# One whole matmul for two half-wide ones in the last Fourier stage of the first batch, with its pieces placed later

## The chip, the cores and the metric

The kernel runs on one core of a Trainium2 chip, as one launch. The metric is the device time of that core in microseconds, median of three runs. A core has five engines with queues of their own: TensorE (PE in the profile; its weight loads are PEld), VectorE (DVE), ScalarE (ACT), GpSimd (POOL) and SyncE (SP, which here only starts DMA transfers). Each works through its queue in order, and they wait for one another through semaphores. Operands lie in SBUF, which has 128 partitions; TensorE writes to PSUM, and DVE and ACT empty PSUM ("evacuate" it).

## The reference

Eight batches of 3008 tokens with 256 channels pass through a global filter (a real Fourier transform along the tokens, a product with a complex filter, the inverse transform) and then through a two-layer network whose activation is h + sin²(αh)/α:

```python
def _attn_ref(x, filt_r, filt_i):                 # x: (8, 3008, 256)
    X = np.fft.rfft(x, axis=1)
    F = (filt_r + 1j * filt_i)[None, :, :]
    return np.fft.irfft(X * F, n=x.shape[1], axis=1).astype(np.float32)

def _moe_ref(x, w_in, w_out, alpha):              # x: (24064, 256), w_in: (256, 2048)
    h = x @ w_in
    s = np.sin(alpha * h)
    g = h + s * s / (alpha + 1e-09)
    return (g @ w_out).astype(np.float32)
```

## The kernel before

**The transform.** 3008 = 94 x 32, and the transform is done in steps of matrix products with tables: a first stage over 94 rows, a forward stage over the other index, the product with the filter, an inverse stage, and a last stage that gives back rows of 94 tokens. Results are fp16 in SBUF.

**Batches 1 to 7** (class `Spectral`) go through DRAM between the stages to turn the data: `first` (L180 matmul, L161/L159 evacuation, store to `d1` on SP), `load_t2` (POOL), `forward` (L200), `product` and `cross` (DVE; the copies `xs` between them are started by SP), `inverse` (L231), `load_t4`, and `last`. Their last stage is L258: four matmuls a piece, each with 128 adjacent columns of `t4_h` as weights and 94 columns of a table as the moving operand.

**Batch 0** is done first, by code of its own, without DRAM in between. Its data stand as pairs of channels, two fp16 values in four bytes, so that DVE's 32x32 transpose (`turn`, L385) can turn pairs as 32-bit words. `pairs(t)` is the view of a tile as partition, s (32), channel pair, k (2): neighbouring channel pairs of one s lie 64 elements (128 bytes) apart, and the two members of a pair lie side by side. The stages:

- 16 matmuls `pa_0` (L371), evacuated by DVE and ACT in turn into `t1_0` as pairs of the channels 2c and 2c+1
- four transposes into `t2_0`, one half of the channels (`hc`) after the other
- twelve blocks of `forward_0` (L403, four matmuls a block over 64 pairs of one half, evacuated by ACT at L407), `product_0` (L412, DVE) and `inverse_0` (L422, eight matmuls a block, evacuated by ACT at L159 into `g_0` as pairs of c and c+64 within the half). Six forward blocks run ahead of the inverse ones; from then on each round has one inverse and one forward block
- `turn_back` (L385, two transposes of 2048 words) into `t4_0`, one half each. These tiles are `t4_h`, which earlier hold half of the turned data (`t2_0[0]`) and the second inverse table (`e1_0`)
- the last stage, 16 pieces `s0.last(u)` of 4 x 94 columns of `y` for 128 channels (L255). A piece takes eight matmuls: for each of four s, the member k of 64 pairs gives the weights, 64 columns wide, and the result goes to PSUM partitions 64k to 64k+63. A piece with `cb` = 0 needs the first `turn_back` alone, one with `cb` = 1 the second. PSUM buffers come from the pool `fps`, which has two. The evacuation goes to ACT or DVE (`on_act`)

`warm_pe(n)` puts n matmuls without use into the queue. `weights_in` (POOL) multiplies the first weights by alpha; `weights_out` (POOL, and ACT for the last four) the second weights by -1/(2 alpha), which `reciprocals` makes from `rec` with a TensorE transpose and a DVE operation.

**The MLP** walks over 48 chunks of up to 512 tokens, 8 steps a chunk. A step issues two hidden blocks (`hidden`: two matmuls at L507, the cosine on ACT at L510, the combination on DVE at L511) and, for the chunk before, projections (`project`, L523; in the first chunk there are none). Hidden blocks have four PSUM buffers (`hps`).

**The order around the change** is written out by hand. `put(at, function)` files a piece of Fourier work under a step number; after the hidden blocks of a step and again after its projections, `slot(step)` and `slot(step + 0.5)` issue what is due, as a rule one piece with matmuls at a time, a second one only when it is a whole step late. Four pieces of batch 0's last stage are issued before the MLP begins; the others are filed in pairs (`last_two`, one piece evacuated by ACT and one by DVE). Chunk 2 (steps 16 to 23) is the first to read pieces 6 to 9.

Of the kernel before, what the change touches and what calls it, by code (L numbers as in the profile page):

```python
# [9 lines left out]
FP16 = mybir.dt.float16  # L10
# [4 lines left out]
ALU = mybir.AluOpType  # L15
# [3 lines left out]
B, S, C = 8, 3008, 256  # L19
# [43 lines left out]
def kernel(  # L63
# [10 lines left out]
    nc = tc.nc  # L74
# [17 lines left out]
    def pool(name, bufs, space=None):  # L92
        kw = {} if space is None else {"space": space}
        return ctx.enter_context(tc.tile_pool(name=name, bufs=bufs, **kw))

    cpool = pool("consts", 1)
# [12 lines left out]

    wf_t = cpool.tile([NR, NK], FP16)  # L110
    t1_h = [cpool.tile([128, 16, C], FP16, name=f"t1_h{i}") for i in range(2)]
    t4_h = [cpool.tile([128, 16, C], FP16, name=f"t4_h{i}") for i in range(2)]

    def by_half(t):

# [8 lines left out]
    for h in range(2):  # L124
        nc.sync.dma_start(out=x32[:, 4 * C * h:4 * C * h + 4 * C],
                          in_=bass.AP(tensor=x.tensor, offset=x.offset + 4 * h * C, ap=[[32 * C, 96], [1, 4 * C]]))
# [4 lines left out]
    wi0_t = cpool.tile([128, NR], FP16)  # L131
    filt_t = cpool.tile([128, 2, NS, C], FP16)
# [23 lines left out]
    def evac(dst, src, on_act=None):  # L156
        flip[0] = (flip[0] + 1) % 3
        if flip[0] if on_act is None else on_act:
            marks["act"] = nc.scalar.copy(out=dst, in_=src)  # L159
        else:  # L160
            marks["dve"] = nc.vector.tensor_copy(out=dst, in_=src)  # L161

    class Spectral:
# [82 lines left out]
        def last(self, u, on_act=None):  # L246
            ch, rest = divmod(u, 4)
            half, cb = divmod(rest, 2)
            n0 = 8 * ch + 4 * half
            ps = fps.tile([128, 4, 128], FP32, name=f"pd_{self.b}_{u}", tag="f")  # L250
            psv = ps.rearrange("p a b -> p (a b)")[:, 0:4 * NR].rearrange("p (a r) -> p a r", r=NR)
            for i in range(4):
                if self.b == 0:
                    for k in range(2):
                        nc.tensor.matmul(out=psv[64 * k:64 * k + 64, i, :], lhsT=t4_0[cb][:, n0 + i, :, k],  # L255
                                         rhs=wi0_t, start=True, stop=True)
                else:
                    nc.tensor.matmul(out=psv[:, i, :], rhs=wi_t, start=True, stop=True,  # L258
                                     lhsT=t4_h[ch // 2][0:NK, n0 % 16 + i, cb * 128:cb * 128 + 128])
            evac(y[:, cb, self.b % 2, n0:n0 + 4, :], psv, on_act)  # L260
# [9 lines left out]
    al = cpool.tile([16, 128], FP32)  # L270
# [33 lines left out]
    for g in range(2):  # L304
        gs = slice(12 * g, 12 * g + 12)
        for k, filt in enumerate((filt_r, filt_i)):
            for q in range(2):
                if (g, k, q) == (0, 1, 1):
# [3 lines left out]
                    out=f_t[k][64 * k + 32 * q:64 * k + 32 * q + 32, gs, :],  # L312
                    in_=bass.AP(tensor=filt.tensor, offset=filt.offset + off,
                                ap=[[N1 * C, 32], [step, 12], [1, C]]))
# [6 lines left out]
    def pairs(t):  # L321

        return t.rearrange("p a (b s k) -> p s (a b) k", s=32, k=2)

    t1_0 = vpool.tile([128, 32, C], FP16, name="t1_0", tag="v")
    t2_0 = [t4_h[0], vpool.tile([128, 16, C], FP16, name="t2_0", tag="v")]
    for hc in range(2):
        nc.vector.memset(pairs(t1_h[hc])[:, NS:32], 0.0)
    t1_0, t2_0, g_0, t4_0 = pairs(t1_0), [pairs(t) for t in t2_0], [pairs(t) for t in t1_h], [pairs(t) for t in t4_h]
    rec = cpool.tile([16, 128], FP32)  # L330
    rec_t = cpool.tile([128, 16], FP32)
# [17 lines left out]
    def warm_pe(n):  # L349

        warmed.append(n)
        ps = hps.tile([128, 512], FP32, name=f"warm_{len(warmed)}", tag="h")
        for i in range(n):
            nc.tensor.matmul(out=ps, lhsT=idle[:, 0:128], rhs=idle[:, 0:512], start=True, stop=True)
# [7 lines left out]
    def cast_x0(h):  # L362

        cs = slice(4 * C * h, 4 * C * h + 4 * C)
        evac(x0[0].rearrange("p n c -> p (n c)")[:, cs], x32[0:NR, cs], False)

    cast_x0(0)
    for i in range(16):
        own, tag = (fps, "f") if i % 3 == 2 else (hps, "h")
        ps = own.tile([128, 512], FP32, name=f"pa_0_{i}", tag=tag)  # L370
        nc.tensor.matmul(out=ps, lhsT=wf0_t[0:NR], rhs=x0[i // 4][:, 2 * (i % 4):2 * (i % 4) + 2, :],  # L371
                         start=True, stop=True)
        evac(t1_0[:, 2 * i:2 * i + 2], ps.rearrange("p (n c k) -> p n c k", n=2, k=2), i % 2)
        if i == 1:
            warm_pe(3)
            cast_x0(1)
        if i < 15 and i % 4 == 3:
            warm_pe((2, 2, 2, 1)[i // 4])
# [9 lines left out]
    def turn_back(hc):  # L388

        turn(t4_0[hc], g_0[hc])  # L390
# [6 lines left out]
    xf0, p0 = {}, {}  # L397

    def forward_0(i):
        hc, w = blocks[i]  # L400
        ps = hps.tile([128, 4, 128], FP32, name=f"pb_0_{i}", tag="h")
        for j in range(4):
            nc.tensor.matmul(out=ps[:, j, :], lhsT=d_t[:, 4 * w + j, :],  # L403
                             rhs=t2_0[hc][:, 4 * w + j], start=True, stop=True)
        own, tag = (xspool, "xs") if i % 2 else (xfpool, "xf")
        xf0[i] = own.tile([128, 4, 128], FP16, name=f"xf_0_{i}", tag=tag)
        nc.scalar.copy(out=xf0[i], in_=ps)  # L407

    def product_0(i):
        hc, w = blocks[i]  # L410
        p0[i] = xpool.tile([128, 2, 4, 128], FP16, name=f"p_0_{i}", tag="x")
        marks["products"] = nc.vector.tensor_tensor(  # L412
            out=p0[i], in0=xf0[i][:, None].to_broadcast([128, 2, 4, 128]),
            in1=filt_t[:, :, 4 * w:4 * w + 4, 128 * hc:128 * hc + 128], op=ALU.mult)

    def inverse_0(i):
        hc, w = blocks[i]
# [36 lines left out]
    s0 = Spectral(0)  # L454

    [inverse_table(g) for g in range(2)]
    for i in range(6):
        forward_0(i)
        if i % 3 == 2:
            if i == 2: inverse_table(2)  # L460
            warm_pe((4, 0)[i // 3])
    for i in range(13):
        for e in {5: [(1,0,False)],6: [(1,1,False)]}.get(i, ()):
            other_half(*e)
        if i < 12:
            product_0(i)
        if i > 0:
            inverse_0(i - 1)
        if i + 6 < 12:
            forward_0(i + 6)  # L470
        if i == 12:
            turn_back(0)
    turn_back(1)
    nc.vector.reciprocal(out=rec, in_=al)
    def weights_out(jb, n=4):

        if n == 1:
            nc.scalar.mul(w2[:, jb, :], w_out32[:, jb, :], rec_t[:, jb:jb + 1])
        else:
            nc.gpsimd.tensor_tensor(out=w2[:, jb:jb + n, :], in0=w_out32[:, jb:jb + n, :],  # L480
                                    in1=rec_t[:, jb:jb + n, None].to_broadcast([128, n, C]), op=ALU.mult)
# [2 lines left out]
    spread_alpha(3)  # L484
    for step in ([(weights_in, g) for g in range(6)] + [(s1.load_x, 0), (s1.load_x, 1)]):
        step[0](*step[1:])
    warm_pe(2)
    s0.last(0, True)
    s0.last(2, True)
    warm_pe(3)  # L490
    s0.last(1, True)
    s0.last(3, False)

    chunks = [(pb, c0, 384 if c0 == 2560 else 512) for pb in range(B // 2)
              for c0 in [*range(0, 2561, 512), *range(2944, 2 * S, 512)]]
# [61 lines left out]
    def put(at, fn, *args, pe=False):  # L557
        pending.append((at, len(pending), pe, fn, args))
# [10 lines left out]
    for i in range(2):  # L569
        put(13 + i, negate, i)  # L570
    for u in range(4, 16, 2):
        put((1,3,4.5,6,14,16)[u // 2 - 2], s0.last_two, u, pe=True)
    for b in range(1, B):
        s = s1 if b == 1 else Spectral(b)
        z = 48 * b
        if b > 1:
            for ch in range(4):
                put((22,27,32,37)[ch] if b == 2 else z - 92 + 7 * ch, s.load_x, ch)
        for i in range(16):
            put(7.5 + 0.3 * i if b == 1 else 36 + 0.66 * i if b == 2 else z - 67 + 0.66 * i, s.first, i, pe=True)  # L580
        for g in range(4):
            put(12.5 if b == 1 else max(z - 56, 46.5), s.load_t2, g)
        for u in range(12):
            inv = 23.5 + 1.25 * u if b == 1 else 59 + 2.1 * u if b == 2 else z - 40.8 + 2.3 * u
            fwd = inv - (6 if b == 1 else 6)
            put(fwd, s.forward, u, pe=True)
            put(fwd + (0.5 if b == 1 else 1.5), s.product, u)
            if s.fused:
                put(fwd + (4 if b == 1 else 4.5), s.cross, u)
            put(inv, s.inverse, u, pe=True)  # L590
        for ch in range(4):
            put(z - (9.5 if b == 1 and ch < 3 else (10.5, 10.5, 10.5, 3)[ch]), s.load_t4, ch)
        for u in range(16):
            put(z + (u - (5 if b == 1 else 6.5) if u < 4 else 2 * u - 9), s.last, u, pe=True)
# [68 lines left out]
```

## Time and profile before

| | us |
|---|---|
| median of three runs | 790.48 (790.2 to 791.0) |
| span of the profiled execution | 789.0 |
| TensorE busy in the span | 776.2 |
| VectorE busy | 657.4 |
| ScalarE busy | 617.0 |
| GpSimd busy | 79.7 |
| L255, 128 matmuls of 64 wide weights | 9.8 |
| L403, 48 matmuls | 6.6 |

The span runs from the first instruction of the program to the last; the time of a run has some work around it, here 1.48 us between the span and the median. A busy TensorE is an upper bound, because matmuls overlap and their ends are modelled; where the distance between starts is known, it is the better price. "L255" is line 255 of the kernel.

### The profile page before, as it was taken

To read this page: it belongs to the slowest core of one execution; us is meant where nothing else is said; L and a number is where in the kernel's file an instruction comes from. 1 tells how busy PE (TensorE), PEld (TensorE's weight loads), DVE (VectorE), ACT (ScalarE), POOL (GpSimd) and SP (SyncE) were. 2 spreads that over 40 slices of the span, in tenths; PEclk is the share of its full clock that TensorE was granted. 3 is DMA by queue.
4 is the path that set the end of the run, shared out by engine and by line. 5 is a ranking of instruction groups with operands and counts; after the bars stand their busy time and mean duration, and the time that the engine had idled before them with its cause. 6 is when DMAs were issued, how large, how long until landed. Compare 5 with 4: busy or idle time off the path is not lost.

```text
span 789.0 us, 16730 instructions
## 1 busy us (share of the span) xinstructions
PE 776.2 (98%) x5854; PEld 536.3 (68%) x5854; DVE 657.4 (83%) x1171; ACT 617.0 (78%) x1209; POOL 79.7 (10%) x125
## 2 busy tenths in 40 slices
PE   8999989999999999999999999999999999999997
PEld 4756757676667766777666766777666776766666
DVE  7887987899878997799978998799987999777773
ACT  6887868888878887888887888788887887777663
POOL 6442000200020000200020000200002000000000
PEclk9999999999999999999999999999999999999999
DMA  9956568755573646554575455845566233421111
GB/s 217 257 105 173 118 144 206 173 104 134 140 198 82 135 98 191 150 121 102 121 210 124 100 106 137 219 94 113 128 165 171 62 97 82 116 62 29 41 41 54
DMA packets 87677, 101.01 MB, mean 128 GB/s; under 512 B 14472, under 2 KB 75928, under 8 KB 87592
## 3 DMA queue, kind: packets, MB, share of 16 engines
q1 hardware_dynamic: 78016, 73.73, 34.5%
q0 software_dynamic: 9360, 26.15, 17.4%
q8 instruction: 46, 0.75, 0.4%
q14 instruction: 39, 0.32, 0.1%
q10 hardware_dynamic: 216, 0.05, 0.0%
HBM read 55.72 MB, written 46.66 MB: 130 GB/s over the span
## 4 chain that ended last, share of the span: by engine, by line
PE 90%; DVE 2%; DMA 2%; ACT 2%; issue 1%; POOL 1%; SPq 1%; ACTq 0%; POOLq 0%; DVEq 0%
PE po L523 40%; PE ph L507 40%; PE pa L180 3%; PE pd L258 2%; PE pb L200 2%; PE pc L231 2%; DMA e_t<-e_tbl 1%; DVE v L511 1%; PE pd L255 1%; DMA xs<-xf 1%; ACT cos_all L510 1%; DVE t_h L385 1%; SPq L549 1%; ACT t_h L159 1%; DVE t_h L161 0%
## 5 line engine op out<-in xcount | busy, mean ns | idle before, releaser
L511 DVE SCALAR_TENSOR_TENSOR v<-cos_all,ph 128x512 f16<-128x512 f32 (+1 forms) x768 | 482.8, 671 | 107.4 <-ACT cos_all L510 103.9
L510 ACT ACTIVATE cos_all<-ph 128x512 f32<-128x512 f32 (+1 forms) x768 | 410.9, 592 | 99.5 <-PE ph L507 98.3
L523 PE MATMUL po<-w,v 128*128 128x256 f16 x3008 | 388.7, 272 | 0.0
L507 PE MATMUL ph<-y,w 128*128 128x512 f16 (+1 forms) x1536 | 386.4, 374 | 0.5 <-DVE y L161 0.3
L523 PEld LDWEIGHTS <-v 128*128 128x128 f16 x3008 | 289.3, 98 | 78.2 <-issue 1.2
L507 PEld LDWEIGHTS <-w 128*128 128x128 f16 x1536 | 147.5, 98 | 104.5 <-issue 2.5
L529 ACT COPY o<-po 128x512 f32<-128x512 f32 (+1 forms) x97 | 55.6, 573 | 19.6 <-PE po L523 12.6
L203 ACT CAST xf<-pb 128x512 f16<-128x512 f32 x84 | 50.0, 595 | 15.2 <-PE pb L200 13.8
L192 POOL DMA_DIRECT2D t<-d x56 | 36.3, 666 | 202.4 <-DMA out_dram<-o 128.6
L159 ACT CAST t_h<-pa 96x512 f16<-96x512 f32 x74 | 43.3, 586 | 8.5 <-PE pa L180 8.3
L140 POOL DMA_DIRECT2D x<-in_x_dram x32 | 17.1, 535 | 302.1 <-PE pc L231 171.4
L159 ACT CAST y<-pd 128x376 f16<-128x376 f32 x83 | 40.0, 482 | 7.6 <-PE pd L258 5.3
L258 PEld LDWEIGHTS <-t_h 96*128 96x128 f16 x448 | 31.4, 97 | 18.4 <-issue 0.4
L180 PE MATMUL pa<-x,wf_t 94*96 94x512 f16 x112 | 42.2, 381 | 1.0 <-DVE t_h L161 0.6
L159 ACT CAST g<-pc 128x512 f16<-128x512 f32 x58 | 34.4, 593 | 9.4 <-PE pc L231 9.0
L221 DVE TENSOR_TENSOR p<-p,xs 128x512 f16<-128x512 f16 x84 | 35.7, 425 | 2.9
L220 DVE TENSOR_TENSOR xs<-xs,filt_t 128x512 f16<-128x512 f16 x84 | 35.0, 416 | 2.8 <-DMA xs<-xf 2.8
L258 PE MATMUL pd<-wi_t,t_h 96*128 96x94 f16 x448 | 37.1, 204 | 0.0
L214 DVE TENSOR_TENSOR p<-xf,filt_t 128x512 f16<-128x512 f16 x84 | 35.0, 416 | 0.0
L231 PE MATMUL pc<-p,e_t 128*128 128x256 f16 x168 | 32.1, 273 | 1.7 <-DVE p L221 1.7
L200 PE MATMUL pb<-t,d_t 128*128 128x256 f16 x168 | 32.1, 272 | 0.5 <-DVE g L161 0.4
L161 DVE CAST t_h<-pa 96x512 f16<-96x512 f32 x38 | 25.9, 681 | 0.7 <-PE pa L180 0.5
(66 smaller groups left out, 257.5 us busy)
## 6 DMA issues: line engine op xcount, KB each, us to landing
x<-in_x_dram POOLq DMA_DIRECT2D x30, 376.0 KB, 5.0
d<-t_h SPq DMA_DIRECT2D x28, 384.0 KB
t<-d POOLq DMA_DIRECT2D x56, 192.0 KB, 4.6
xs<-xf SPq DMA_DIRECT2D x168, 64.0 KB
d<-g SPq DMA_DIRECT2D x56, 192.0 KB
t_h<-d SPq DMA_DIRECT2D x28, 384.0 KB
out_dram<-o SPq DMA_DIRECT2D x104, 80.0 KB
w_out<-in_moe_w_out_dram SPq DMA_DIRECT2D x1, 2048.0 KB
```

What stands on the lines that cost most here:

```text
L159: marks["act"] = nc.scalar.copy(out=dst, in_=src)
L180: marks["pe"] = nc.tensor.matmul(out=ps[0:NK, :], lhsT=wf_t, rhs=self.x[ch][:, 2 * j:2 * j + 2, :], start=True, stop=True)
L192: nc.gpsimd.dma_start(out=self.t2[g][64 * p:64 * p + 64, :, :], in_=self.d1[a0:a0 + 6, :, :].rearrange("s n c -> n s c"))
L200: nc.tensor.matmul(out=ps[:, i, :], lhsT=d_t[:, s, :], rhs=self.t2[s // 6][:, s % 6, :], start=True, stop=True)
L203: nc.scalar.copy(out=self.xf[u], in_=ps)
L231: nc.tensor.matmul(out=ps[:, i, :], lhsT=e_t[:, 2 * w + i, :], rhs=pt[:, i, :], start=(k == 0), stop=(k == len(pr) - 1))
L258: nc.tensor.matmul(out=psv[:, i, :], rhs=wi_t, start=True, stop=True, lhsT=t4_h[ch // 2][0:NK, n0 % 16 + i, cb * 128:cb * 128 + 128])
L507: nc.tensor.matmul(out=ps[:, 0:n], lhsT=w1[:, cb, jb * 128:jb * 128 + 128], rhs=y_cols[:, cb, c0:c0 + n], start=(cb == 0), stop=(cb == 1))
L510: nc.scalar.activation(out=cs[:, 0:n], in_=ps[:, 0:n], func=AFT.Sin, bias=float(np.pi / 2))
L511: marks["snake"] = nc.vector.scalar_tensor_tensor(out=v[k][:, jb, 0:n], in0=cs[:, 0:n], scalar=-1.0, in1=ps[:, 0:n], op0=ALU.add, op1=ALU. ...
L523: nc.tensor.matmul(out=pso[k][:, t % 2, :], lhsT=v[k][:, jb, 128 * t:128 * t + 128], rhs=w2[:, jb, :], start=(jb == 0), stop=(jb == 15))
L529: nc.scalar.copy(out=o[:, i0:t % 2 + 1, :], in_=pso[k][:, i0:t % 2 + 1, :])
```

## The change

The diff does five things. The pairs of batch 0 become the channels c and c+128 (the evacuation of `pa_0`, the order in which `forward_0` reads, the columns of the filter in `product_0`). Both halves of `t4` become one tile, so that one member k of all 128 pairs can be the weights of one matmul, and a piece takes four matmuls rather than eight. With that every piece needs both `turn_back` transposes; the four early pieces are issued in order, with ACT and DVE in turn, after eight warm matmuls in one group, and the reciprocal is issued after them on DVE. The pairs of pieces from 4 on are filed at 2, 5, 13, 14.5, 16 and 17.5 rather than at 1, 3, 4.5, 6, 14 and 16. Batch 1's first stage is filed from 7.9 rather than from 7.5.

```diff
-    t4_h = [cpool.tile([128, 16, C], FP16, name=f"t4_h{i}") for i in range(2)]
+    t4_a = cpool.tile([128, 2, 16, C], FP16)
+    t4_h = [t4_a[:, i] for i in range(2)]
...
                 if self.b == 0:
-                    for k in range(2):
-                        nc.tensor.matmul(out=psv[64 * k:64 * k + 64, i, :], lhsT=t4_0[cb][:, n0 + i, :, k],
-                                         rhs=wi0_t, start=True, stop=True)
+                    nc.tensor.matmul(out=psv[:, i, :], lhsT=t4_cols[:, n0 + i, :, cb], rhs=wi0_t,
+                                     start=True, stop=True)
...
+    t4_cols = t4_a.rearrange("p h a (b s k) -> p s (h a b) k", s=32, k=2)
...
-        evac(t1_0[:, 2 * i:2 * i + 2], ps.rearrange("p (n c k) -> p n c k", n=2, k=2), i % 2)
+        evac(t1_0[:, 2 * i:2 * i + 2], ps.rearrange("p (n k c) -> p n c k", n=2, k=2), i % 2)
...
-                             rhs=t2_0[hc][:, 4 * w + j], start=True, stop=True)
+                             rhs=t2_0[hc][:, 4 * w + j].rearrange("p c k -> p k c"), start=True, stop=True)
...
-            out=p0[i], in0=xf0[i][:, None].to_broadcast([128, 2, 4, 128]),
-            in1=filt_t[:, :, 4 * w:4 * w + 4, 128 * hc:128 * hc + 128], op=ALU.mult)
+            out=p0[i].rearrange("p f s (k c) -> p f s k c", k=2),
+            in0=xf0[i].rearrange("p s (k c) -> p s k c", k=2)[:, None].to_broadcast([128, 2, 4, 2, 64]),
+            in1=filt_t[:, :, 4 * w:4 * w + 4].rearrange("p f s (k c) -> p f s k c", k=2)[..., 64 * hc:64 * hc + 64],
+            op=ALU.mult)
...
-    nc.vector.reciprocal(out=rec, in_=al)
...
-    warm_pe(2)
-    s0.last(0, True)
-    s0.last(2, True)
-    warm_pe(3)
-    s0.last(1, True)
-    s0.last(3, False)
+    warm_pe(8)
+    for u in range(4):
+        s0.last(u, u % 2 == 0)
+    nc.vector.reciprocal(out=rec, in_=al)
...
-        put((1,3,4.5,6,14,16)[u // 2 - 2], s0.last_two, u, pe=True)
+        put((2,5,13,14.5,16,17.5)[u // 2 - 2], s0.last_two, u, pe=True)
...
-            put(7.5 + 0.3 * i if b == 1 else 36 + 0.66 * i if b == 2 else z - 67 + 0.66 * i, s.first, i, pe=True)
+            put(7.9 + 0.3 * i if b == 1 else 36 + 0.66 * i if b == 2 else z - 67 + 0.66 * i, s.first, i, pe=True)
```

## The prediction

> **What bounds the kernel now.** I read the page first, then the chain of waits in order of time over the first 75 us, then the timeline of the matmuls that the change touches, then the busy times of the first MLP chunk.
>
> The page (busy microseconds, share of the span, number of instructions; then the chain that ended last):
>
> ```profile
> span 789.0 us, 16730 instructions
> PE 776.2 (98%) x5854; PEld 536.3 (68%) x5854; DVE 657.4 (83%) x1171; ACT 617.0 (78%) x1209; POOL 79.7 (10%) x125
> PE 90%; DVE 2%; DMA 2%; ACT 2%; issue 1%; POOL 1%; SPq 1%; ACTq 0%; POOLq 0%; DVEq 0%
> ```
>
> TensorE is busy 98% and is 90% of the chain. What moves the end is therefore either matmul time in the saturated part or delay ahead of it. The chain (start, length, what):
>
> ```profile
> 11.77 9.71 DMA e_t<-e_tbl
> 21.53 0.64 PE pc L422 x8
> ...
> 29.75 0.61 ACT t_h L159
> 30.38 4.51 DVE t_h L385 x2
> 34.94 1.23 PE pd L255 x16
> 36.19 0.56 DVE y L161
> 36.79 0.82 PE ph L507 x3
> ...
> 65.79 1.11 PE pd L255 x15
> 70.48 1.09 PE pd L255 x16
> ```
>
> Until 21.53 us the chain is a DMA (`e_t`). Then come the evacuations of the first batch's inverse stage (L159), the two `turn_back` transposes (L385), the first four pieces of the last stage (L255) and the MLP, which begins to flow at 36.79. Pieces 12 to 15 (at 65.79 and 70.48) lie on the chain by themselves, some 1.1 us a pair of pieces.
>
> The timeline (start, duration, engine, line; "xN" merges N equal instructions, and the duration includes the last one's latency):
>
> ```profile
> 15.70 1.49 PE L403 MATMUL pb<-t_h,d_t 128*128 128x128 f16 x12
> 17.12 0.64 PE L343 MATMUL pse<-id,d_t 128*64 128x128 f16 x16
> 17.69 1.04 PE L354 MATMUL warm<-idle 128*128 128x512 f16 x4
> 21.99 0.60 PE L403 MATMUL pb<-t,d_t 128*128 128x128 f16 x4
> 22.41 0.23 PE L422 MATMUL pc<-p,e_t 128*128 128x128 f16 x1
> 38.68 1.23 PE L255 MATMUL pd<-wi_t,t_h 128*64 128x94 f16 x16
> 137.60 0.33 PE L258 MATMUL pd<-wi_t,t_h 96*128 96x94 f16 x4
> ```
>
> The busy times of the first MLP chunk (stretch, its length; PE, weight loads, DVE, ACT, POOL busy with their instructions; granted clock, DMA share, GB/s):
>
> ```profile
> 36.79:50.13 13.34, 12.52 (x97) 7.40 (x98) 10.55 (x19) 10.48 (x22) 10.60 (x9) 1.00 0.73 152
> ```
>
> Three prices follow. L403 streams 128 columns as 64 adjacent pairs, each pair 128 bytes from the next: (1.49 - 0.29) / 11 = 0.11 us a matmul. L422 streams 128 adjacent columns: the eight of the chain give (0.64 - 0.22) / 7 = 0.06. L255 runs its 64-wide halves two and two: (1.23 - 0.30) / 7.5 = 0.12 us a pair. With its first load, which nothing hides, and the return to L507, a pair of pieces takes about 1.2. L258, the later batches' whole matmul with adjacent weight columns, takes (0.33 - 0.20) / 3 = 0.043. The first chunk takes 13.34 us, in which PE, DVE and ACT are busy 12.52, 10.55 and 10.48. There the matmuls of four pairs of pieces alternate with ACT and DVE. The granted clock is 1.00, so no price is a clock effect.
>
> **The change, part by part.** The sum is made against the profiled span of 789.0 us; the median of the runs is 790.48, so 1.48 lies around the span and is carried over.
>
> *A. The rearranged forward (L403 before).* The channel pairs are now c and c+128. To that end 48 forward matmuls read "k c": 128 single columns, each 128 bytes from the last, where pairs were read before. The trace has no such moving read. Lower bound: 0.11 each, as now (even less is excluded: it touches the same places with shorter runs). Upper bound: if a place costs what a pair costs now, 0.11 / 64 = 1.7 ns, 128 of them take 0.22. The nearest row is the strided weight load of L255, single columns at the same step: 0.12 for 64, or 1.9 ns a column, again a price for each place visited. I take 0.22. TensorE then runs 12 x 0.22 = 2.65 from 15.70, the transposes and the warm matmuls 0.57 + 0.86 until 19.8, and four blocks of 0.88 until 23.35. The first inverse starts there and not at 21.53; the wait for `e_t` was the cover, and it is used up. Five rounds of 0.44 (inverse) + 0.88 (forward) bring inverse 5 to 30.0 (25.96 now). ACT then empties inverses 5 to 9 at 0.62 each from 30.65, so the first `turn_back` can start at 33.75 and not at 30.38: **+3.4** (bounds 0 and 3.4). `weights_in` on POOL is queued behind the products and starts some 2.7 later; its six operations take 9.65 and then the weights of the second projection follow. These have over 2 us to spare now (POOL idles 2.33 us at 39.64).
>
> [...]
>
> The other edits here cost nothing that I count. The 16 evacuations of L371 read PSUM in another order at 9 to 13 us, under the `e_t` DMA; L159 takes 636 ns in the first batch's inverse, which reads PSUM so, and 593 in the later ones'; a growth of that size is hidden as well. The 12 products have the same elements in runs of 64 (0.62 each now). The copies and DMAs of the filter do not change.
>
> *B. The start of the MLP.* Pieces 0 and 2 ran between the two transposes. Now all four wait for the second one, and `warm_pe(8)` ends before it does. Four pieces share two PSUM buffers (`fps`), so pieces 2 and 3 wait for evacuations of 0.47 (ACT) and 0.55 (DVE). With a whole matmul at price r: at r = 0.043 the fourth evacuation ends 37.35, at 0.12 it ends 38.0, against 36.75 now. I take **+0.9** (bounds 0.6 and 1.3). The reciprocal (0.90, on DVE at 34.80 now) goes behind the evacuations; it lies in DVE's wait for the first cosine, and TensorE's transpose of `rec` waits for it some 0.25, which is in C.
>
> *C. The first chunk.* Two pairs of pieces leave it. DVE has 16 x 0.64 (L511) + 2 x 0.55 + 0.17, ACT 16 x 0.55 + 2 x 0.48 + 4 x 0.47: both about 11.5, and TensorE under 9. From the second hidden matmul, DVE starts 1.05 later and needs 9.6 until the buffer for the next chunk's first hidden matmul is free, plus about 0.3 of gaps. That makes 10.95 where 13.34 are spent now: **-2.4** (bounds -1.9, -2.6).
>
> *D. The pieces in the saturated part.* Four pairs lie there and not two. A pair costs 8r and 0.1 at its edges. Bounds for r: 0.043 (L258, adjacent columns) and 0.145 (no gain: 1.16 us for eight pairs of halves, which load the same 128 columns at the same step). Between them I take 0.08: the whole load is L258's shape with L255's addresses, and lies near neither. Then 4 x 0.75 - 2 x 1.2 = **+0.6** (bounds -0.7 and +2.6).
>
> [...]
>
> *E. The later start of batch 1's first stage.* Its matmuls, evacuations, and the DMAs on SP (d1 out) and POOL (t2 in) move about half a step, and so does the first forward (its slot goes to pieces 14 and 15). Their distance stays: 0, with 1.5 either way, since the stall now at 115 us (1.46 behind one cross product, which waits for a copy queued on SP behind stores) can shrink or grow.
>
> Sum: 3.4 + 0.9 - 2.4 + 0.6 = **+2.5**: span 791.5, median **793.0**.
>
> **Rivals.** *1. The single-column read costs what the pair read does* (A = 0). For it: the time could be one per element, 128 at 0.8 ns. Against it: L255's loads, where 64 elements take as long. The sum is -0.9: 789.6. With r at L258's 0.043, D becomes -0.7 and B 0.6, the sum -2.5: 788.0. This is the case on the other side: its place is 15 to 30 us, its price 0 for 3.4, and it decides as soon as a forward matmul takes under about 0.15 us, since then the wait for `e_t` covers it. *2. The whole weight load gains nothing* (r = 0.145). For it: the same addresses are visited. Against it: a wide load at another odd step (L300, one column repeated) takes no more than an adjacent one, 98 ns on the record. With A at 3.4: 3.4 + 1.3 - 2.2 + 2.6 = +5.1, or 795.6.
>
> **Numbers.** The forecast has a chance of 0.50, its own range is 791.5 to 795.0. Rival 1 has 0.34, rival 2 0.16. A measurement here tells a change from none at about 0.2%, 1.6 us. Of the forecast 0.42 is slower and 0.08 within; of rival 1 0.19 faster, 0.14 within, 0.01 slower; rival 2 is slower. So 0.19 faster, 0.22 within, 0.59 slower. The range 788.0 to 796.0 leaves out E's ends in both directions.
>
> **What would show it.** A is right if the forward matmuls start 0.2 us apart and the first `turn_back` starts near 33.7; at 0.11 apart and 30.4, rival 1 holds. B is right if the second hidden matmul starts about 2.8 us after the second transpose's end (1.9 now), and wrong under 2.2 or over 3.5. C: next chunk's first matmul some 11 us after it. D: eight L255 matmuls take about 0.75, or 1.2 for rival 2. A new wait over 2 us between 50 and 120 us, or a first inverse held by a filter copy rather than by TensorE, would make the sum wrong.

## The result and the profile after

The changed kernel takes 794.64 us (median of 10 runs), the kernel before 790.89 beside it (10 runs): a ratio of 1.0042, with a 95% interval from 1.0025 to 1.0058. The profiled spans are 792.4 and 789.0, 3.4 us apart, where 2.5 was forecast; the forecast median was 793.0.

The page of the changed kernel, with the lines that were shown of before:

```profile
span 792.4 us, 16609 instructions
PE 779.4 (98%) x5793; PEld 535.6 (68%) x5793; DVE 658.8 (83%) x1172; ACT 617.6 (78%) x1208; POOL 80.0 (10%) x125
PE 90%; DVE 4%; DMA 2%; ACT 2%; issue 1%; SPq 0%; POOL 0%; ACTq 0%; POOLq 0%
```

TensorE has 61 matmuls fewer on record (64 fewer of the last stage, three more warm ones) and is busy 3.2 us longer. The chain of waits in order of time (start, length, what; L404 is the forward, L403 before; L425 the inverse, L422 before; L386 the transposes, L385 before):

```profile
3.98 10.81 DMA id<-id
...
15.91 2.72 PE pb L404 x12
...
20.17 3.48 PE pb L404 x16
23.65 0.45 PE pc L425 x8
...
34.76 4.52 DVE t_a L386 x2
...
39.33 0.57 PE pd L255 x4
...
40.45 0.92 PE pd L255 x8
41.39 0.56 DVE y L162
41.99 1.39 PE ph L507 x3
...
68.95 0.69 PE pd L255 x8
...
70.51 0.33 PE pd L255 x4
...
71.39 0.48 PE pd L255 x4
...
74.47 0.68 PE pd L255 x8
...
77.76 0.69 PE pd L255 x8
```

The chain now runs through the forward matmuls; the wait for `e_t` is no longer in it. The first `turn_back` starts at 34.76 (30.38 before), the second hidden matmul at 41.99 (36.79). A pair of pieces in the saturated part takes 0.69 rather than 1.1, and there are four of them, one cut in two by a wait for an evacuation on ACT.

The timeline of the changed matmuls:

```profile
15.87 2.77 PE L404 MATMUL pb<-t_a,d_t 128*128 128x128 f16 x12
46.22 0.82 PE L255 MATMUL pd<-wi_t,t_a 128*128 128x94 f16 x8
```

A forward matmul takes (2.77 - 0.39) / 11 = 0.217 us (0.11 before), a whole last-stage matmul (0.82 - 0.26) / 7 = 0.08 within the burst, and 0.087 with its edges (0.69 / 8).

Busy times of three stretches of the changed kernel (stretch, its length; PE, weight loads, DVE, ACT, POOL; granted clock, with 1.00 as full speed, DMA share, GB/s):

```profile
41.99:53.34 11.35, 10.36 (x48) 4.86 (x48) 10.07 (x18) 9.49 (x20) 9.07 (x9) 0.85 0.72 111
25.00:28.40 3.40, 3.40 (x28) 2.68 (x26) 3.20 (x4) 2.51 (x5) 0.00 (x0) 0.50 0.81 212
42.00:45.40 3.40, 3.40 (x9) 1.14 (x9) 2.41 (x5) 1.79 (x3) 2.88 (x5) 0.51 0.26 20
```

The first chunk takes 11.35 us (13.34 before). The last two rows show something the profile of the kernel before, with a mean clock of 1.000, doesn't have: for two stretches of 3.4 us TensorE's clock is at half (0.50 and 0.51).

Three marks in the trace make a ledger: the end of the second `turn_back`, the first hidden matmul of the next chunk (the 33rd of L507), and the end.

| us | before | after | difference | forecast |
|---|---|---|---|---|
| until the second `turn_back` ends | 34.9 | 39.3 | +4.4 | +3.4 |
| from there to the next chunk | 15.25 | 14.07 | -1.2 | -1.5 |
| from there to the end | 738.9 | 739.0 | +0.1 | +0.6 |

The last row is no sharp test. The profiles of e1, e3, e5 and e7 below have the same code behind the second mark and took 739.9, 740.1, 739.1 and 739.3 there, so that one profile against another tells nothing under about 1 us in this stretch.

### The profile page after: what moved, and what is told of

It reads as the page before. It is cut to its first block, busy times and chain, and to the rows that moved or that the text cites. A ratio compares the mean times of both kernels' runs of the same rounds, so it can differ in the third digit from the quotient of the medians.

```text
span 792.4 us, 16609 instructions
## 1 busy us (share of the span) xinstructions
PE 779.4 (98%) x5793; PEld 535.6 (68%) x5793; DVE 658.8 (83%) x1172; ACT 617.6 (78%) x1208; POOL 80.0 (10%) x125
## 3 DMA queue, kind: packets, MB, share of 16 engines
q0 software_dynamic: 9360, 26.15, 17.5%
## 4 chain that ended last, share of the span: by engine, by line
PE 90%; DVE 4%; DMA 2%; ACT 2%; issue 1%; SPq 0%; POOL 0%; ACTq 0%; POOLq 0%
PE po L523 39%; PE ph L507 39%; PE pa L181 3%; PE pd L258 2%; PE pb L201 2%; PE pc L232 2%; DVE v L511 2%; DMA id<-id 1%; PE pb L404 1%; ACT cos_all L510 1%; DVE t_a L386 1%; PE pd L255 1%; PE pc L425 1%; DMA t_a<-d 0%; SPq L549 0%
## 5 line engine op out<-in xcount | busy, mean ns | idle before, releaser
L507 PE MATMUL ph<-y,w 128*128 128x512 f16 (+1 forms) x1536 | 387.9, 376 | 1.3 <-DVE v L511 1.0
L507 PEld LDWEIGHTS <-w 128*128 128x128 f16 x1536 | 148.2, 98 | 106.2 <-issue 5.4
L529 ACT COPY o<-po 128x512 f32<-128x512 f32 (+1 forms) x97 | 55.7, 575 | 19.6 <-PE po L523 12.9
L258 PEld LDWEIGHTS <-t_a 96*128 96x128 f16 x448 | 31.3, 97 | 19.9 <-DMA t_a<-d 1.5
L181 PE MATMUL pa<-x,wf_t 94*96 94x512 f16 x112 | 42.3, 381 | 0.3
L258 PE MATMUL pd<-wi_t,t_a 96*128 96x94 f16 x448 | 37.1, 204 | 1.2 <-DMA t_a<-d 1.2
L162 DVE CAST y<-pd 128x376 f16<-128x376 f32 x46 | 25.0, 543 | 3.4 <-PE pd L258 1.7
```

Source lines behind the costliest of these rows:

```text
L181: marks["pe"] = nc.tensor.matmul(out=ps[0:NK, :], lhsT=wf_t, rhs=self.x[ch][:, 2 * j:2 * j + 2, :], start=True, stop=True)
L507: nc.tensor.matmul(out=ps[:, 0:n], lhsT=w1[:, cb, jb * 128:jb * 128 + 128], rhs=y_cols[:, cb, c0:c0 + n], start=(cb == 0), stop=(cb == 1))
L529: nc.scalar.copy(out=o[:, i0:t % 2 + 1, :], in_=pso[k][:, i0:t % 2 + 1, :])
```

## The experiments

All times stand beside runs of the kernel before on the same chips. The ledger's stretches are worked out from each trace in the same way.

**e1: the pair read again.** The changed kernel, with the forward reading pairs in place.

```diff
-                             rhs=t2_0[hc][:, 4 * w + j].rearrange("p c k -> p k c"), start=True, stop=True)
+                             rhs=t2_0[hc][:, 4 * w + j], start=True, stop=True)
...
-        nc.scalar.copy(out=xf0[i], in_=ps)
+        nc.scalar.copy(out=xf0[i].rearrange("p s (k c) -> p s k c", k=2),
+                       in_=ps.rearrange("p s (c k) -> p s k c", k=2))
```

> The changed kernel, but forward_0 reads the pairs in place (c k) again, and ACT puts them into the order (k c) while it empties PSUM. Theory (the single-column read sets the early delay): forward matmuls return from 0.217 to 0.11 us, the first inverse waits for e_t again at about 21.5, the clock of 0.50 between 25 and 28.4 us is gone, the first turn_back starts at 30.4 to 30.8 and not at 34.76, and the span falls by about 4, from 792.4 to 788 to 789: ratio to the kernel before 0.997 to 1.000. Rival (the loss comes from the four early pieces and the new places of the others; the read is hidden): turn_back moves by under 1 us or the gain is used up before the MLP, ratio stays 1.003 to 1.005. If ACT's strided read of PSUM costs more than 0.1 us a block, turn_back starts nearer 31.5.

Measured: 789.92 us, ratio 0.9986 (0.9970 to 1.0002), span 789.0. The first transpose in the chain of waits of this run:

```profile
31.73 4.51 DVE t_a L386 x2
```

In this run the first forward started at 17.23, 1.36 later than in the changed kernel (15.87), because the first tables landed later. From the first forward to the first `turn_back` it is 14.5 us, against 18.9 in the changed kernel and 14.7 before. So the early delay is gone, and ACT's reordering costs nothing that shows in it. The clock is 1.00 from 14 to 59 us. The theory holds, the rival falls. Two of its signs were missed: `turn_back` starts after the stated 30.4 to 30.8, though 31.73 less the 1.36 would lie at 30.4, and the first inverse, at 22.45, waits for no `e_t`. The two marks show that the read isn't all of the 3.4 us between the two spans: the second transpose ends 3.0 us earlier than in the changed kernel, the next chunk follows 1.2 sooner (12.90 and not 14.07, at full clock), and the rest takes 0.85 longer.

**e2: the single-column read by itself**, in the kernel before.

```diff
-                             rhs=t2_0[hc][:, 4 * w + j], start=True, stop=True)
+                             rhs=t2_0[hc][:, 4 * w + j].rearrange("p c k -> p k c"), start=True, stop=True)
...
-        nc.scalar.copy(out=xf0[i], in_=ps)
+        nc.scalar.copy(out=xf0[i].rearrange("p s (c k) -> p s c k", k=2),
+                       in_=ps.rearrange("p s (k c) -> p s c k", k=2))
```

> The kernel before with one part of the change alone: forward_0 reads 128 single columns (k c), and ACT restores the old order while it empties PSUM. Theory: forward matmuls take 0.217, turn_back starts between 33.8 and 34.8 (30.4 before), and as nothing else is won the whole delay reaches the end: plus 3.5 to 4.5 us, ratio 1.0045 to 1.0055. If the half clock at 25 us comes from this read and not from the rest of the change, it shows here as well. Rival (read hidden): ratio 1.000 to 1.001.

Measured: 794.78 us, ratio 1.0051 (1.0031 to 1.0071). This one part makes the kernel as slow as the whole change does. Stretches of this run (columns as above), then its chain:

```profile
17.20:20.60 3.40, 3.40 (x36) 1.79 (x30) 3.37 (x4) 3.32 (x5) 1.95 (x3) 0.99 1.17 181
20.60:24.00 3.40, 3.40 (x16) 1.61 (x13) 2.90 (x5) 1.83 (x3) 0.00 (x0) 0.50 1.26 195
27.40:30.80 3.40, 3.40 (x26) 2.69 (x25) 3.17 (x5) 2.39 (x5) 0.00 (x0) 0.50 0.68 179
30.80:34.20 3.40, 3.40 (x38) 2.49 (x37) 1.72 (x3) 2.72 (x6) 0.00 (x0) 1.00 0.97 300
```

```profile
26.83 0.85 PE pb L403 x4
27.67 0.86 PE pc L423 x8
...
31.54 0.86 PE pb L403 x4
32.40 0.45 PE pc L423 x8
...
37.48 4.52 DVE t_h L385 x2
```

The clock is at half from 20.6 to 30.8 although TensorE is busy without a gap from 17.2 on. A forward block takes 0.85 at half clock and 0.86 at the full one, while an inverse block (L423) takes 0.86 and 0.45: in these two rows the single-column read sets the forward's pace and not the clock. From the first forward (17.35) to `turn_back` (37.48) this run needs 20.1 us, 1.2 more than the changed kernel, whose clock was at half for one such stretch there and not three.

So the cause is confirmed, and two sizes are missed. `turn_back` starts at 37.48 and not between 33.8 and 34.8; 1.65 of that is a later first forward (15.70 before), the rest lies in the 20.1. And the whole delay doesn't reach the end: the second transpose ends 7.1 us later than before (41.99 against 34.88), the span is 5.0 longer (794.0). The stretch behind the second mark is 2.1 shorter, most of it idle time of TensorE; the wait of 1.46 that the kernel before has at 115.5 us isn't in this trace.

**e3: more warm matmuls.** `warm_pe(8)` becomes `warm_pe(12)` in the changed kernel, nothing else.

> The changed kernel with twelve warm matmuls rather than eight ahead of the four pieces, which fills TensorE's idle 0.87 us before the second turn_back ends. Theory (the clock of 0.51 between 42 and 45.4 us follows from the idle stretch before it): the clock stays 1.00 there, the first hidden matmuls run at 0.216 rather than 0.427 us, and the MLP's first chunk ends about 1 us earlier: ratio 1.0025 to 1.0035. Rival (the clock has another cause, or DVE hides the slow matmuls): the clock stays halved, or it recovers and the span stays within 0.3 of 792.4.

Measured: 795.27 us, ratio 1.0046 (1.0026 to 1.0065), span 794.2. The times that ran at half clock in the changed kernel:

```profile
42.00:45.40 3.40, 2.89 (x18) 1.58 (x18) 2.42 (x4) 1.84 (x4) 3.40 (x4) 1.00 0.01 3
```

The clock stayed at 1.00 there, and the second mark follows the first by 12.9 us and not by 14.07: 1.2 won, as expected. That the four matmuls did it isn't shown by this one profile, because e1 kept its clock there with eight; the last section counts all executions.

The ratio was missed. The profiled execution lost its clock elsewhere, at 0.50 from 20.1 to 30.3 us, and needed 20.1 us from first forward to `turn_back`, as in e2. But it had the lowest clock of the nine (0.994, the others 0.996 to 1.000), so it doesn't explain their median. Why the 1.2 don't show in the ratio stays open.

**e4: two halves for each whole matmul**, all else as changed.

```diff
-                    nc.tensor.matmul(out=psv[:, i, :], lhsT=t4_cols[:, n0 + i, :, cb], rhs=wi0_t,
-                                     start=True, stop=True)
+                    for k in range(2):
+                        nc.tensor.matmul(out=psv[64 * k:64 * k + 64, i, :],
+                                         lhsT=t4_cols[:, n0 + i, 64 * k:64 * k + 64, cb],
+                                         rhs=wi0_t, start=True, stop=True)
```

> The changed kernel with two half-wide matmuls again in place of each whole one, everything else as changed. Theory (the whole load saves TensorE 0.12 - 0.087 a matmul, and its edges): a pair of pieces takes 1.2 and not 0.7, four pairs lie in the saturated part, so plus 2.0, and plus 0.3 to 0.5 at the start of the MLP: span 794.5 to 795, ratio 1.006 to 1.0075. Rival (TensorE has room where the pieces lie): ratio 1.004 to 1.005 as the changed kernel.

Measured: 798.17 us, ratio 1.0090 (1.0069 to 1.0112), span 794.6. Two of its late pairs of pieces on the chain (L256 is L255 here):

```profile
77.04 1.08 PE pd L256 x16
80.84 1.11 PE pd L256 x13
```

So a whole matmul does save 0.4 us a pair of pieces, and the rival falls. The span is in the stated range, the ratio above it: 0.0048 or 3.8 us over the changed kernel's where the spans are 2.2 apart. The profiled execution was the fastest of its six (796.46, median 798.17). Behind the second mark, in the changed kernel and in e4:

```profile
53.34:792.38 739.04, 732.45 (x5440) 508.24 (x5439) 618.37 (x1115) 581.54 (x1147) 50.11 (x82) 1.00 0.50 122
54.77:794.59 739.82, 734.38 (x5472) 509.42 (x5471) 618.15 (x1115) 581.48 (x1147) 50.22 (x82) 1.00 0.50 122
```

TensorE is busy 1.9 us longer, close to the 2.0 expected; the stretch grew by 0.8 only, because e4 lacks waits that the changed kernel has there (1.24 us for batch 1's `t4` at 132 us is the largest).

**e5: pair read and twelve warm matmuls together.**

> The changed kernel with the pair read of the first experiment and twelve warm matmuls. Theory: both losses of clock are gone, whatever the phase of the clock; from the end of the second turn_back to the next chunk's first hidden matmul 12.9 us, as in the two runs that kept the full clock there, against 15.25 before and 14.06 in the changed kernel. Ratio to the kernel before 0.996 to 0.999. Rival (the warm matmuls delay the pieces or change nothing): the same as the pair read alone, 0.9986, or more.

Measured: 788.66 us, ratio 0.9981 (0.9965 to 0.9998), from mark to mark 12.91. But the clock of the profiled execution wasn't safe:

```profile
19.00:22.40 3.40, 2.06 (x17) 1.66 (x16) 3.09 (x6) 3.28 (x6) 0.00 (x0) 1.00 1.22 205
22.40:25.80 3.40, 3.13 (x30) 3.13 (x31) 2.55 (x5) 1.86 (x4) 0.00 (x0) 0.52 0.46 110
```

Here TensorE idled in the stretch before (2.06 busy of 3.40, with the DMA share at 1.22), and the next one ran at half clock (0.52). This was the slowest of the 12 executions (790.71, clock 0.998); the others have 0.999 to 1.000. The ratio is in the stated range, but its interval also holds the 0.9986 of the pair read alone.

**e6: pair read, and every piece at its old place** (1, 3, 4.5, 6, 14, 16 and batch 1 from 7.5; eight warm matmuls).

> The changed kernel with the pair read, and with the pieces and batch 1's first stage at their places of before (1, 3, 4.5, 6, 14, 16 and 7.5). Theory (parts C and D): two pairs of pieces go back into the first chunk, where DVE and ACT set the pace: the stretch from the second turn_back to the next chunk grows from 12.9 by about 1.0 (two evacuations each, 0.55 and 0.48), and two pairs of 0.69 leave the saturated part: minus 1.4. Net minus 0.4 against the pair read alone, ratio 0.997 to 0.9995. Rival (moving the pieces is what wins): the stretch grows by 2 or more, ratio 1.000 to 1.002.

Measured: 791.43 us, ratio 1.0008 (0.9990 to 1.0027), 0.0022 or 1.7 us above e1, with intervals that overlap. The theory fails here, and the rival's ratio is met. From mark to mark 14.69 (12.9 in e1): 1.8 more, not 1.0. And what was to come back later didn't:

```profile
75.04 0.38 PE L201 MATMUL pb<-t,d_t 128*128 128x256 f16 x2 [2.48 <-DMA t<-d]
...
77.58 1.91 PE L508 MATMUL ph<-y,w 128*128 128x512 f16 x4
```

Batch 1's first forward waits 2.48 us for its data from DRAM, and the four hidden matmuls after that take 1.91 rather than 1.03: the clock again (0.54 from 77 to 80 us). In the changed kernel, pieces that stand behind batch 1's first stage lie in this time. That they are what covers the load, and not the start at 7.9, is borne out by e8: it starts the first stage at 7.5 again, with the pieces at their new places, and its first forward has no such wait.

**e7: e5, and pieces 2 and 3 with PSUM buffers of their own.**

```diff
-            ps = fps.tile([128, 4, 128], FP32, name=f"pd_{self.b}_{u}", tag="f")
+            own, tag = (hps, "h") if self.b == 0 and u in (2, 3) else (fps, "f")
+            ps = own.tile([128, 4, 128], FP32, name=f"pd_{self.b}_{u}", tag=tag)
```

> As e5, and pieces 2 and 3 take their PSUM buffers from the pool of the hidden blocks, so that they do not wait for the evacuations of pieces 0 and 1. Theory (part B is set by two buffers): from the second turn_back's end to the second hidden matmul 2.1 us and not 2.7; half of it reaches the end: ratio 0.0005 below e5. Rival (the evacuations set the start by themselves, one after the other on ACT and DVE): 2.5 to 2.7, no change.

Measured: 788.28 us, ratio 0.9967 (0.9949 to 0.9985). The chain of this run (L256 and L509 are L255 and L507):

```profile
34.62 1.63 PE pd L256 x16
...
36.88 0.39 PE ph L509
...
47.05 0.59 PE ph L509 x2
```

The four pieces run without a gap in 1.63 us. From the second transpose (34.56) to the second hidden matmul it is 2.32 (2.72 in the changed kernel, 2.1 expected), from mark to mark 12.48 against 12.91 in e5. So the theory holds for most of the step. This version is 0.3% faster than the kernel before, and its interval leaves out 1; from e5 the ratio doesn't tell it apart.

**e8: e7, with batch 1's first stage from 7.5 again.**

> As e7, with batch 1's first stage filed from 7.5 again. Theory (part E: the shift of 0.4 steps keeps all distances): the first forward of batch 1 doesn't wait for t2, the span stays within 1 us of e7's 786.3, ratio 0.9955 to 0.998. Rival (the shift is needed, because the first chunk has become shorter: the weights of the second projection or the x loads on POOL come too late for an earlier start): a new wait of over 0.5 us at the first matmuls of L181, or of L201 as in e6, and a ratio over 0.998.

Measured: 789.27 us, ratio 0.9988 (0.9974 to 1.0002), span 786.8 and 12.51 from mark to mark. The span is within 0.5 us of e7's, the ratio is outside what was expected, with an interval that overlaps e7's. No forward waits for `t2` and the span stays, as the theory has it. But both signs of the rival came too: a ratio over 0.998, and waits of 0.7 and 0.6 us at L181 that e7 doesn't have, though for evacuations and not for weights or loads (the kernel before, with the same 7.5, has one of 0.6). What the 0.4 steps are worth stays open.

## Why the prediction was right, step by step

**A, the single-column read.** Right in cause, and 1.0 too small. The 0.22 us a matmul came out as 0.217: 128 places at 1.7 ns, the price that the pair read has for each of its 64. The first inverse started at 23.47 (23.35 forecast). The five rounds to inverse 5 then took 7.35 us and not 6.6, because 25.0 to 28.4 ran at half clock (an inverse block took up to 0.85 there, and 0.45 outside), which no term of the sum had. Without these 0.75 the first `turn_back` would have started, by estimate, within 0.3 of the forecast 33.75. e1 and e2 show the cause from both sides: take the read away and the delay goes, put it alone into the kernel before and the delay comes.

**B, the start of the MLP.** 2.72 us from the transpose to the second hidden matmul, 2.8 forecast. e7 confirms that the two buffers are part of it: 0.4 us.

**C, the first chunk.** Mis-sized. 10.95 us were forecast and 11.35 measured, but with TensorE at half clock for 3.4 of them; at full clock it is 10.17 in e1, e3 and e5. So at full clock the gain was 3.2 and not 2.4, and the clock took 1.2 of it back. The sum counted the evacuations that leave with two pairs of pieces. e6, with all pairs back, takes 11.93: 1.8 of the 3.2 came by moving the pairs, and 1.4 are there with the pieces at their old places, for which the sum has no term. The whole loads are a candidate; at the new places, though, the chunk takes no longer with halves (11.30 in e4, also partly at half clock). The cause of the 1.4 stays open.

**D, the pieces in the saturated part.** The price of 0.08, chosen between 0.043 and 0.145, was met at 0.080 to 0.087; e4 shows that the gain over halves is real (1.08 and 1.11 a pair of pieces there). With columns 128 bytes apart a whole matmul costs about twice the 0.043 that L258's takes with adjacent columns in the kernel before. The four pairs took 2.9 (0.69, 0.33 and 0.48, 0.68, 0.69), and one wait of 0.56 for an evacuation stands between the halves of the second.

**E, distances.** The waits behind cross products (1.7 us in all, the 1.46 at 115.5 us among them) shrank to 0.2, and a new one of 1.24 for batch 1's load of `t4` came at 132. They nearly cancel, inside the 1.5 allowed, and that is luck: the wait for `t4` was 2.19 in e1 and 0.2 in e5, with the same code there. And "their distance stays" hid that the moved pieces cover the load of `t2`, which e6 showed.

**The sum.** The half clock cost about 0.75 in A and 1.2 in C, and no term had it. That the total is off by 0.9 and not by 1.7 is luck: C's gain at full clock was 0.8 larger than forecast.

**Rivals.** Rival 1 (a single column costs no more than a pair) falls with 0.217. Rival 2 (no gain from the whole load) falls with 0.69 against 1.1.

## What to carry to other kernels

Here a layout that makes one operand better was paid for where it is read: a whole matmul saved 0.4 us a pair of pieces, and the price was 48 matmuls whose moving operand lost its last adjacent pair (0.217 us each rather than 0.11). Put a strided step on the engine that has time for it; ACT took the reordering at no cost that showed in e1 (its first three evacuations of forward blocks take 1.56 us, as in the kernel before). When work is moved to where an engine is saturated, ask also which transfer it used to cover or now covers (2.48 us of waiting for a load in e6).

## What the runs showed of the hardware

TensorE's granted clock fell to 0.50 for stretches of 3.4 us, and the edges lie on one grid: 25.0, 28.4, 42.0 and 45.4 in the changed kernel are multiples of 3.4 apart. The clock fell after stretches that were far from idle: 2.06 of 3.40 busy in e5, and 3.40 of 3.40 in e2 (17.2 to 20.6, then 0.50), where the forward matmuls read single columns. Busy time alone doesn't decide it, since e1 kept 1.00 through and after this one, with 2.18 of 3.41:

```profile
26.83:30.24 3.41, 2.18 (x32) 1.80 (x31) 3.28 (x6) 3.03 (x7) 0.00 (x0) 1.00 0.74 192
```

Each execution has its mean clock on record. By estimate, one stretch of 3.4 us at half clock in 790 us brings it to 0.998 (0.5 x 3.4 / 790 is 0.002), which is the mean of the profiled executions of e5 and e6; so a mean under 0.999 tells of about one or more, wherever it lay (in the profile of e6 it was at 77 us):

| kernels | forward reads | warm matmuls there | executions under 0.999 |
|---|---|---|---|
| before, beside the experiments | pairs | 2 and 3 | 18 of 66 |
| e2 | single columns | 2 and 3 | 6 of 6 |
| changed, e4 | single columns | 8 | 16 of 16 |
| e3 | single columns | 12 | 8 of 9 |
| e1, e6 | pairs | 8 | 16 of 24 |
| e5, e7, e8 | pairs | 12 | 3 of 36 |

So with the single-column read nearly every execution loses clock (30 of 31), and with the pair read and twelve warm matmuls most keep it (33 of 36; e1 against e5, which differ in four of these matmuls alone, but ran on different chips: 7 of 12 and 1 of 12). No trace shows what lowers the clock; that it is the slow stream of single columns (0.217 us a matmul, against 0.11 for pairs and 0.06 for adjacent columns) is an inference from these runs.
